# The first two products of a last second layer, taken as one two-level Strassen unit

## The chip, the cores and the metric

The kernel runs on one core of one Trainium2 chip. The metric is the device time of one execution in microseconds; the figure given for a kernel is the median of its runs. The profile times instructions on TensorE (PE, with PEld for its weight loads), VectorE (DVE), ScalarE (ACT), GpSimd (POOL) and on SyncE's queue (SP), which issues nearly all DMAs here.

## The reference

Eight batches of 576 tokens go through an efficient attention of eight heads; the result, as a 576 x 512 matrix x per batch, goes through a Fourier mixing block with a two-layer MLP:

```python
def _attn_ref(q, k, v):            # (8, 8, 576, 64) each
    q_s = softmax over the last axis;  k_s = softmax over the sequence axis
    kv = np.einsum('bhsd,bhse->bhde', k_s, v)
    return np.einsum('bhsd,bhde->bhse', q_s, kv)

def _moe_ref(x, w_ch1, w_ch2):     # x (8, 576, 512)
    mixed = np.real(fft(fft(x, axis=1), axis=2))
    u = x + mixed
    un = (u - mean(u)) / np.sqrt(var(u) + 1e-06)
    ch = np.maximum(un @ w_ch1, 0.0) @ w_ch2     # 512 -> 2048 -> 512
    return u + ch
```

All is fp32. This document is about the two matrix products of the MLP: the first layer (`un @ w_ch1`, then the ReLU) and the second layer (`@ w_ch2`).

## The kernel before

The 8 x 576 tokens are cut into nine groups of 512 rows. They are worked through in turn, and a group's place in the turn is called its order, 0 to 8 (B = 8). Each group has a first and then a second layer, and TensorE goes from one to the next without a break. This document needs **order 7** (`B - 1`) and **order 8** (`B`, the last).

**Strassen, one and two levels.** From order 1 on, each layer is done as the seven products of Strassen's scheme in Winograd's form instead of eight. A layer's left and right matrices are cut into 2 x 2 blocks; block sums ("sides") are made ahead, the seven products are numbered 1 to 7 and taken in the order `ORDER = (1, 6, 5, 7, 2, 4, 3)`, and their results are added up with running sums called s1, u2, u3. In the second layer products 1, 2 and 4 take raw blocks of the hidden layer and 7, 5, 6, 3 take sums of them; of the weights 1, 2 and 3 take raw blocks. Some products are cut once more in the same way, into seven sub-products; two products so treated together are a two-level *unit*.

- *First layer, order 7 and 8* (`wide_up`). Four *parts* j = 0..3, each for one pair of 128-row slices of the hidden layer in two halves. A part does products 1, 6, 7, 5 (`SHORT`) plainly, each as 8 matmuls of 128x256 in the records (line 1687). Products 2, 3 (and 4) are done for all parts at once as two-level units by `wide_unit`, seven sub-products of 8 matmul records of 128x128 each (line 1636). `WIDE` says which: `(2, 3)` in order 7, so there product 4 is done plainly in every part, and `(2, 3, 4)` in order 8. The TensorE order is part 0, the units, parts 1, 2, 3. A unit's results lie in the hidden layer's slots `WIDE_AT` until a part adds them (`more`, line 1698, on GpSimd). Then ReLU on ScalarE (line 1716), then the sides of the second layer (`side`, line 1701): slots 4, 2 on VectorE and 5, 6 on GpSimd, all four on VectorE for the last part.
- *Second layer, order 2 to 8* (`deep_down`). Order 7: product 1 plainly (`single`, line 1845: 32 matmul records of 128x256), then units (2, 4), (7, 6), (5, 3). Order 8: products 1 and 2 plainly, then units (7, 6), (5, 3), then product 4 plainly. A unit's sub-products (line 1875) are 16 matmul records of 128x128 for the two products together. VectorE makes a unit's sides (`a_step`, line 1821), adds up its results (`ends` and `plus`, line 1882), and adds results to x (`into`, line 1825; `add`, line 1856).

**PSUM.** Eight banks: one each named ba, bb, bc and one, and four that these layers do not use. Each of the first four has one buffer: a new group in a bank waits until what was in it has been read. The two-level units of the second layer put sub-products 1, 2 into ba, 6, 7, 4 into bb, 5, 3 into bc, so that a unit ends in bc and the next begins in ba.

**Weights.** They are streamed by SP through four slots of 1 MB, in the order of `self.plan`; `used(n)` frees a slot and issues the load of entry n + 4 (`load`, line 481). `w2d` in DRAM holds the ready sub-blocks of products 2 to 7, `w2s` the blocks for the plain form.

**Order of work.** Every step has a time written by hand, relative to its layer's begin (a part's or a unit's time is in nominal units, scaled by 0.87 for orders 1 to 8). All steps are sorted by it, and each engine does its own in that order; waits come from data dependencies alone. So an engine's queue is in strict order: an instruction that waits holds up all behind it on that engine. In order 8's first layer part 0 begins at 0, the units at 8, 15.2 and 22.4, parts 1 to 3 at 29.6, 37.6 and 45.6, the second layer at 53.6.

Of the kernel before, what the change touches and what calls it, by code (L numbers as in the profile page):

```python
# [141 lines left out]
class _Block:  # L142
    def __init__(self, ctx, tc, q, kT, v, w1, w2, ft, cd, out):
# [331 lines left out]
    def load(self, n):  # L475

        if n >= len(self.plan):
            return
        k = (n + 3) % 4
        w = self.big[:, k * NP * HD:(k + 1) * NP * HD]  # L480
        self.nc.sync.dma_start(w[:, :self.plan[n].shape[1]], self.plan[n])
        self.stream[n] = w.rearrange("p (a n) -> p a n", n=HD)
# [1132 lines left out]

    def wide_unit(self, g, m, e, *at_sums):
# [51 lines left out]
    def wide_up(self, order, g):  # L1668

        nc, V, G = self.nc, self.nc.vector, self.nc.gpsimd  # L1670
        base, wide = self.base[order], WIDE[order]
        products = [m for m in (*SHORT, 4) if m not in wide]
        size = 2 * len(products)

        def part(t, j, done):
# [3 lines left out]
            def product(m, i):  # L1679
                name = {1: "ba", 6: "bb", 7: "one", 5: "bc", 4: "one"}[m]  # L1680
                if i == 0 and m == 7:
                    box[name] = self.acc((P, D)).rearrange("p (j n) -> p j n", n=HD)
                elif i == 0 and m != 4:
                    box[name] = self.ps.tile([P, 2, HD], F32, tag=name, name=name)[:]
                w = self.stream[base + 2 * j + i]
                for k in range(2):
                    nc.tensor.matmul(box[name][:, i, :], lhsT=w[:, WA_AT[m], k * P:(k + 1) * P], rhs=self.unT[g][:, B_AT[m], k, :],  # L1687
                                     start=m != 4 and i == 0 and k == 0, stop=k == 1, skip_group_check=True)
# [8 lines left out]
            def more(to, of, m):  # L1697
                G.tensor_tensor(out=hp(to), in0=of(), in1=hp(WIDE_AT[m]), op=ALU.add)
# [7 lines left out]
            def late(m, i):  # L1706
                put(done[m] - t, more, i, own(i), m)
                put(done[m] - t + 1.6, relu, i)

            def sides(t, by_pool, last):  # L1710
                put(t, side, V, 4, 2, 3, ALU.add)
                put(t + 0.05, side, V, 2, 0, 2)
                put(by_pool, side, V if last else G, 5, 4, 0)
                put(by_pool + 0.1, side, V if last else G, 6, 1, 5)
# [4 lines left out]
            last, own_third = j == NP // 2 - 1, j == 0 and 4 in wide  # L1719
            for k, m in enumerate(products):  # L1720
# [4 lines left out]
            put(3.9, lambda: plus(temp("u2"), "bb", own(0) if j == 0 else got("s1")))  # L1725
            put(5.9, lambda: plus(hp(1) if own_third else temp("u3"), "one", got("u2")))
            put(7.9, lambda: plus(hp(3), "bc", own(1) if own_third else got("u3")))
            put(8.8, relu, 3)
            if j == 0:
                put(8.7, lambda: plus(hp(2), "bc", got("u2")))  # L1730
            else:
                put(4.7, lambda: more(WIDE_AT[3], got("u2"), 3))
                put(8.7, lambda: plus(hp(2), "bc", own(WIDE_AT[3])))
            if 4 not in wide:
                put(size - 0.1, lambda: plus(hp(1), "one", got("u2")))
                put(size + 0.7, relu, 1)
            if j == 0:
                put(1.9, lambda: nc.scalar.copy(hp(0), box["ba"]))
                for m, i in ((2, 0), (3, 2), (4, 1)):
                    if m in wide:  # L1740
                        late(m, i)
                t = max(done.values())
                sides(2.6, 3.4, False)
                return steps
            put(1.9, lambda: nc.scalar.copy(temp("s1"), box["ba"]))
            put(1.95, lambda: plus(hp(0), "ba", own(WIDE_AT[2])))
            put(2.8, relu, 0)
            if 4 in wide:
                put(6.7, lambda: more(1, got("u3"), 4))
                put(8.4 if last else size + 2.2, relu, 1)  # L1750
            put(9.5 if last and 4 in wide else size + 2.1 - 1.5 * last, relu, 2)
# [6 lines left out]
        t, units, done = size, [], {}  # L1758
        for k, m in enumerate(wide):
            e, times = (V, (-5.2, -5.1, -3.1, -3.0) if k else (-3.05, -3, -1.3, -1.2)) if order == B else (  # L1760
                G, [x - t + 0.1 * i for i, x in enumerate([10.1 if k else 0.5] * 4)])
            units += at(t, self.wide_unit(g, m, e, *times))
            t += UNIT
            done[m] = t + 0.5
        steps = part(0, 0, done) + units
        for j in range(1, NP // 2):
            steps += part(t, j, done)
            t += size
# [26 lines left out]
    def deep_down(self, g, order):  # L1795
# [4 lines left out]
        late, order = order == B - 2, (1, 2, *UNITS[1:], 4) if last else (1, *UNITS)  # L1800
# [3 lines left out]
        temps = {4: lambda i: un(i), 2: lambda i: un(3 + i), 7: self.gap, 6: dead(1), 5: (lambda i: un(i)) if last else dead(4), 3: (lambda i: un(3 + i)) if last else dead(2)}  # L1804
        result = {m: self.hblock(A_AT[m], 0, 0) for m in A_AT}
        tile = lambda m: result[m].rearrange("p (c e) n -> p c e n", c=2)
        box, steps, late_second = {}, [], not last and E is V
# [4 lines left out]
        def own(m):  # L1812
            def get(i):
                return temps[m](i - 4) if i > 3 else self.hblock(A_AT[m], i // 2, i % 2)
            return get

        def a_step(m, o):
# [3 lines left out]
            e.tensor_tensor(out=to(o), in0=to(x), in1=to(y), op=op)  # L1821
# [40 lines left out]
        place = {1: "ba", 2: "ba", 6: "bb", 7: "bb", 4: "bb", 5: "bc", 3: "bc"}  # L1862

        def product(unit, n, i):
            m = unit[i]
# [5 lines left out]
            if first:  # L1871
                bank(place[n])
            for f in range(4):
                r = q % 4 * 4 + f
                nc.tensor.matmul(box[place[n]][:, i, :], lhsT=own(m)(A_AT[n])[:, f, :],  # L1875
# [7 lines left out]

        def ends(unit, n):
            first, last = (A_AT[m] for m in unit)
            step = last - first
            out = lambda j: self.hpairs(j)[:, first:last + (1 if step > 0 else -1):step, 0:P]
            if n == 1:
                nc.scalar.copy(temp("s1"), box["ba"][:])
# [12 lines left out]
        after = {(2, 4): [(7, into, 1, 0, 4), (9, into, 0, 0, 2)],  # L1902
# [6 lines left out]
        for i, unit in enumerate(order):  # L1909
            if unit in A_AT:  # L1910
                w = base + (i if i < 2 else 2 + (len(DEEP) - skip) // 4)
# [15 lines left out]
            early = 6 if last and t < n + 8 else 0 if t == 8 else t - n + 2 if i == 2 else t - n + (0 if last else 3)  # L1927
            for k, o in enumerate((4, 5, 2, 6)):
                for j, m in enumerate(unit[::-1] if late_second and unit == (2, 4) else unit):
                    put(early + step * k + j * 1.1 + 0.3 + late * (i == 2), a_step, m, o)  # L1930
            for k, o in enumerate(ORDER):
                for j in range(2):
                    put(t + 2 * k + j, product, unit, o, j)
                put(t + 2 * k + 1.5, ends, unit, o)
            t += n
            for dt, *some in after[unit]:
                put(t + dt, *some)
        if last:
# [100 lines left out]
def kernel(ctx: ExitStack, tc: tile.TileContext, q, kT, v, w1, w2, ft,  # L2039
                                                           cd, out):  # L2040
    blk = _Block(ctx, tc, q, kT, v, w1, w2, ft, cd, out)

    ups = lambda order: len(WIDE[order]) * UNIT + 2 * (len(ORDER) - len(WIDE[order])) * (NP // 2) if order in WIDE else UP

    def timed(t, order, g):
# [5 lines left out]
        if order == B - 1:  # L2051
            steps += at(t, blk.wide_sums(3, blk.nc.gpsimd, 10.5, 10.6, 10.7, 10.8) + blk.wide_sums(4, blk.nc.gpsimd, 33, 34.6, 43, 44.6))
# [153 lines left out]
```

## Time and profile before

| | |
|---|---|
| median of 3 runs | 1004.52 us (1004.2 to 1005.18) |
| profiled execution, its own time | 1004.87 us |
| its span, first to last instruction | 1003.0 us |
| granted TensorE clock | 1.000 |
| busy: PE / PEld / DVE / ACT / POOL | 992.3 / 856.7 / 734.3 / 499.0 / 501.2 us |
| order 7, first and second layer | from 814 and from 862 us |
| order 8, first and second layer | from 907 and from 953 us |

Times in rows are microseconds from the span's start. In a timeline row stand the start, the length, the engine, the line, the operation, output and inputs by tile name, the shape and a count; in brackets the idle time before it and what ended it. Consecutive like instructions are merged into one row, so three of 0.6 us read as one row with x3. A matmul row's length holds the drain of its last matmul (0.16 us), so the next row starts before it ends.

### The profile page before, as it was taken

How to read it: one execution, taken by the hardware profiler on the slowest of the kernel's cores; microseconds unless marked ns; L12 is line 12 of the kernel's file. 1: busy time of each engine (PE TensorE's matmuls, PEld its weight loads, DVE VectorE, ACT ScalarE, POOL GpSimd, SP SyncE). 2: the span in 40 equal slices, each digit the busy share in tenths (PEclk: the TensorE clock that was granted, in tenths of full speed). 3: DMA queues.
4: the chain of work that ended last, by engine and by line, in shares of the span. 5: the costliest groups of instructions: out<-in, count | busy, mean ns of one | idle time of the engine just before them, and what ended most of it. 6: DMA issues, size and time to landing. Idle time of an engine off the chain costs nothing.

```text
span 1003.0 us, 20195 instructions
## 1 busy us (share of the span) xinstructions
PE 992.3 (99%) x7682; PEld 856.7 (85%) x7682; DVE 734.3 (73%) x1382; ACT 499.0 (50%) x1287; POOL 501.2 (50%) x492
## 2 busy tenths in 40 slices
PE   8999999999999999999999999999999999999998
PEld 7844464888888899889988998899888999999997
DVE  6898899666765887678756877688656956785673
ACT  5684643862468228842775167725782242252310
POOL 4363420357535637664655566665646396252510
PEclk9999999999999999999999999999999999999999
DMA  9986499687989666975778577947755964675473
GB/s 299 262 291 236 164 258 330 201 242 234 328 293 262 237 229 221 271 238 209 254 219 229 207 267 246 263 168 268 229 189 200 334 230 152 257 267 202 172 262 131
DMA packets 127256, 239.53 MB, mean 239 GB/s; under 512 B 24296, under 2 KB 92136, under 8 KB 116536
## 3 DMA queue, kind: packets, MB, share of 16 engines
q1 hardware_dynamic: 126792, 237.72, 72.5%
q8 instruction: 61, 1.00, 0.4%
q14 instruction: 35, 0.29, 0.1%
q10 hardware_dynamic: 288, 0.26, 0.1%
q0 software_dynamic: 80, 0.26, 0.1%
HBM read 203.08 MB, written 39.06 MB: 241 GB/s over the span
## 4 chain that ended last, share of the span: by engine, by line
PE 85%; DVE 8%; ACT 4%; issue 1%; DMA 1%; SPq 0%; POOL 0%; DVEq 0%; POOLq 0%
PE bb L1551 11%; PE bb L1875 10%; PE ba L1551 8%; PE bc L1551 7%; PE ba L1875 7%; PE bc L1875 7%; PE bb L1845 6%; PE bc L1484 2%; PE one L1687 2%; PE bb L1965 2%; PE two L845 2%; ACT qT L822 2%; PE two L1212 1%; PE two L1269 1%; PE one L760 1%; PE ba L1484 1%
## 5 line engine op out<-in xcount | busy, mean ns | idle before, releaser
L1551 PE MATMUL bb<-unT,big 128*128 128x256 f32 x576 | 137.8, 381 | 0.0
L1551 PEld LDWEIGHTS bb<-unT,big 128*128 128x128 f32 x576 | 108.4, 190 | 15.5 <-DVE u L1519 0.5
L822 ACT ACTIVATE qT<-q 32x128 f32<-32x128 f32 x384 | 117.9, 307 | 5.9 <-DVE q L812 0.8
L1875 PE MATMUL bb<-big 128*128 128x128 f32 x848 | 103.8, 276 | 0.2
L1875 PEld LDWEIGHTS bb<-big 128*128 128x128 f32 x848 | 98.9, 192 | 1.0 <-DVE u L1882 1.0
L1551 PE MATMUL ba<-unT,big 128*128 128x256 f32 x384 | 93.7, 383 | 0.0
L1551 PE MATMUL bc<-unT,big 128*128 128x256 f32 x384 | 91.2, 380 | 0.1
L1825 POOL TENSOR_TENSOR x<-x,big 128x512 f32<-128x512 f32 x45 | 60.7, 1363 | 46.0 <-DVE big L1882 19.7
L1563 ACT ACTIVATE big<-big 128x512 f32<-128x512 f32 x72 | 44.7, 629 | 77.9 <-DVE big L1562 71.3
L1551 PEld LDWEIGHTS bc<-unT,big 128*128 128x128 f32 x384 | 72.5, 190 | 10.4 <-DVE big L1562 0.5
L1519 DVE TENSOR_TENSOR u<-bb,s 128x512 f32<-128x512 f32 x50 | 34.2, 684 | 64.4 <-PE bb L1551 45.9
L1551 PEld LDWEIGHTS ba<-unT,big 128*128 128x128 f32 x384 | 71.3, 190 | 10.6 <-issue 0.5
L1821 DVE TENSOR_TENSOR big<-big 128x512 f32<-128x512 f32 x98 | 79.7, 840 | 0.0
L1875 PE MATMUL ba<-big 128*128 128x128 f32 x640 | 79.0, 276 | 0.0
L1875 PEld LDWEIGHTS ba<-big 128*128 128x128 f32 x640 | 75.0, 192 | 0.8
L809 POOL TENSOR_TENSOR q<-q,qm 128x512 f32<-128x512 f32 x24 | 25.8, 1074 | 89.1 <-DVE qm L804 55.4
L1395 POOL COPY unT<-unT 32x256 f32<-32x256 f32 x98 | 44.1, 450 | 48.1 <-DVE unT L1387 43.8
L1395 ACT COPY unT<-unT 32x256 f32<-32x256 f32 x126 | 50.7, 402 | 31.5 <-DVE unT L1387 29.7
L410 POOL TENSOR_TENSOR big<-big 128x512 f32<-128x512 f32 x24 | 30.5, 1270 | 67.2 <-ACT big L1563 67.2
L1845 PE MATMUL bb<-big 128*128 128x256 f32 x256 | 58.3, 379 | 0.0
L1845 PEld LDWEIGHTS bb<-big 128*128 128x128 f32 x256 | 48.0, 190 | 6.1
L1875 PE MATMUL bc<-big 128*128 128x128 f32 x416 | 50.7, 275 | 0.0
(410 smaller groups left out, 2211.6 us busy)
## 6 DMA issues: line engine op xcount, KB each, us to landing
big<-w2d SPq DMA_DIRECT2D x67, 1024.0 KB
big<-w1s SPq DMA_DIRECT2D x64, 896.0 KB
big<-w2s SPq DMA_DIRECT2D x16, 1024.0 KB
big<-in_w_dram SPq DMA_DIRECT2D x21, 512.0 KB
w2d<-big SPq DMA_DIRECT2D x42, 256.0 KB
kb<-in_kT_dram SPq DMA_DIRECT2D x28, 320.0 KB
q<-in_q_dram SPq DMA_DIRECT2D x28, 256.0 KB
vt<-in_v_dram SPq DMA_DIRECT2D x84, 80.0 KB
```

The costliest lines, as they stand in the source:

```text
L410: e1.tensor_tensor(out=to(4), in0=at(2), in1=at(3), op=ALU.add)
L809: G.tensor_tensor(out=heads(), in0=heads(), in1=m[:].unsqueeze(2).to_broadcast([P, H, DH]), op=ALU.add)
L822: nc.scalar.activation(to[t, i * Q:i * Q + Q], one, ACT.Exp)
L1395: copy(to, of)
L1484: nc.tensor.matmul(po[:], lhsT=h[:, f, i * P:(i + 1) * P], rhs=self.w2sb[:, f, :], start=(f == 0), stop=(f == NF - 1))
L1519: plus = lambda t: V.tensor_tensor(out=temp(t), in0=box["bb"][:], in1=box["s1"][:], op=ALU.add)
L1551: nc.tensor.matmul(bank()[:, i, :], lhsT=w[:, WA_AT[m], k * P:(k + 1) * P], rhs=self.unT[g][:, B_AT[m], k, :], start=first and i == 0 and ...
L1563: (0.8, lambda: nc.scalar.activation(hp(i), hp(i), ACT.Relu))]
L1821: e.tensor_tensor(out=to(o), in0=to(x), in1=to(y), op=op)
L1825: E.tensor_tensor(out=x, in0=x, in1=tile(m), op=ALU.add)
L1845: nc.tensor.matmul(box[name][:, i, :], lhsT=h[p][:, A_AT[m], i * P:(i + 1) * P], rhs=self.stream[n][:, p, :], start=p == 0 and (m != 1 or ...
L1875: nc.tensor.matmul(box[place[n]][:, i, :], lhsT=own(m)(A_AT[n])[:, f, :], rhs=w[:, r // 2, r % 2 * P:r % 2 * P + P], start=first and f == ...
```

## The change

1. **Order 7, first layer.** `WIDE` becomes a list in which parts and units are mixed: `(0, 0), 2, 3, (0, 1), 4, (0, 2), (0, 3)`. Product 4 is a two-level unit there too, between parts 1 and 2. Its weight sides (`wide_sums(4)`, GpSimd) come some 17 nominal units sooner; its activation sides are made by VectorE. Order 8's list is as it was.
2. **First layers of both orders.** `WIDE_AT` puts the units' results in other slots; the times of `sides` are changed, partly by the table `SIDES`; in the last part the addition of product 4 (`more`) moves from GpSimd to VectorE, and its ReLU comes 0.8 sooner. In order 8 the last part's sides come 1.9 later.
3. **Order 8, second layer.** Products 1 and 2 become a two-level unit (1, 2). Its sub-products come in the order `RAW_FIRST = (1, 4, 2, 6, 5, 7, 3)`: 1, 4, 2 take raw blocks of the hidden layer. Sub-product 4 gets bank one and 3 gets bank ba. The unit's eight side steps are on VectorE at 1.55 to 1.7 and 7.6 to 9.7; those of unit (7, 6) begin at 8.3.
4. **Weights for it.** Product 2's come as two stream entries from `w2d`, taken at every other sub-block (2 KB pieces). Product 1's raw block is loaded into `kb` at 16.2 of order 8, and VectorE makes its four sums at 23.2, 25.9, 32.4 and 36.35 (`last_first`).
5. Unit (2, 4) of order 7 makes its sides in the order 2, 4 instead of 4, 2 (`late_second` is gone).

```diff
+RAW_FIRST = (1, 4, 2, 6, 5, 7, 3)
-UNIT, WIDE_AT = 7.2, {2: 5, 3: 6, 4: 4}
-WIDE = {B - 1: (2, 3), B: (2, 3, 4)}
+UNIT, WIDE_AT = 7.2, {2: 4, 3: 5, 4: 6}
+WIDE = {B - 1: ((0, 0), 2, 3, (0, 1), 4, (0, 2), (0, 3)), B: ((0, 0), 2, 3, 4, (0, 1), (0, 2), (0, 3))}
+SIDES = {(B - 1, 0): (25.2, 32, 31, 41), (B - 1, 1): (33.2, 35.2, 34.2, 45.9), (B, 0): (25.1, 28.05, 26.5, 31.7)}
...
-            self.plan += [one(m) for m in (ORDER if at == 1 else (1, 2) if at == B else (1,))]
+            if at == B:
+                self.plan += [self.w2d[:, i:j:2, :] for i, j in ((0, 8), (8, 2 * len(ORDER)))]
+            else:
+                self.plan += [one(m) for m in (ORDER if at == 1 else (1,))]
...
+    def last_first(self, *times):
...
+        def load():
+            raw = kb[:, 0:4 * GT]
+            self.nc.sync.dma_start(raw, self.w2s[WB_AT[1]].rearrange("p a n -> p (a n)"))
...
+        def make(o, x, y):
+            V.tensor_tensor(out=w[o], in0=w[x], in1=w[y], op=ALU.subtract)
+        some = (4, 1, 0), (1, 3, 1), (5, 3, 4), (6, 2, 5)
+        return [(times[0], load)] + [(t, lambda a=a: make(*a)) for t, a in zip(times[1:], some)]
...
-            def more(to, of, m):
-                G.tensor_tensor(out=hp(to), in0=of(), in1=hp(WIDE_AT[m]), op=ALU.add)
+            def more(to, of, m, e=G):
+                e.tensor_tensor(out=hp(to), in0=of(), in1=hp(WIDE_AT[m]), op=ALU.add)
...
-                put(4.7, lambda: more(WIDE_AT[3], got("u2"), 3))
+                put(5.2, lambda: more(WIDE_AT[3], got("u2"), 3))
...
+                put(6.7, lambda: more(1, got("u3"), 4, V if last else G))
+                put(7.6 if last else size + 2.2, relu, 1)
             if last:
-                sides(size + 2.6, size + 3.4, True)
+                late = 1.9 * (order == B)
+                sides(*(size + late + dt for dt in (2.6, 2.65, 3.4, 3.5)), True)
+            elif (order, j) in SIDES:
+                sides(*(x - t for x in SIDES[order, j]))
             else:
-                sides(size + (3.95 if 4 in wide else 2.3), size + (8.3 if 4 in wide else 3), False)
+                sides(size + 2.8, size + 4.75, size + 3.7, size + (6.7 if j == NP // 2 - 2 else 8.2))
...
+        if order == B:
+            steps += self.last_first(16.2, 23.2, 25.9, 32.4, 36.35)
...
-        late, order = order == B - 2, (1, 2, *UNITS[1:], 4) if last else (1, *UNITS)
+        late, order = order == B - 2, ((1, 2), *UNITS[1:], 4) if last else (1, *UNITS)
...
+        def place(unit, n):
+            return {4: "one", 3: "ba"}.get(n, "bb" if n in (6, 7) else "bc" if n == 5 else "ba") if unit == (1, 2) else {1: "ba", 2: "ba", 6: "bb", 7: "bb", 4: "bb", 5: "bc", 3: "bc"}[n]
+        def raw_first(unit, n, i):
...
+        def ends_raw(n, out):
+            if n == 1:
+                nc.scalar.copy(temp("s1"), box["ba"][:])
+            if n == 6:
+                plus(temp("u2"), "bb", "s1")
+            if n == 7:
+                plus(temp("u3"), "bb", "s1")
+                plus(out(3), "bc", "u3")
+                plus(out(2), "one", "u3")
+            if n == 2:
+                nc.scalar.copy(out(0), box["ba"][:])
+            if n == 5:
+                plus(box["u2"][:], "bc", "u2")
+            if n == 3:
+                plus(out(1), "ba", "u2")
...
-            early = 6 if last and t < n + 8 else 0 if t == 8 else t - n + 2 if i == 2 else t - n + (0 if last else 3)
-            for k, o in enumerate((4, 5, 2, 6)):
-                for j, m in enumerate(unit[::-1] if late_second and unit == (2, 4) else unit):
+            early = 8 if last and t < n + 8 else 0 if t == 8 else t - n + 2 if i == 2 else t - n + (0 if last else 3)
+            if unit == (1, 2):
+                for m, at_steps in ((1, (1.55, 1.65, 7.6, 9.6)), (2, (1.6, 1.7, 7.7, 9.7))):
+                    for o, dt in zip((4, 5, 2, 6), at_steps):
+                        put(dt, a_step, m, o, V)
+            for k, o in enumerate((4, 5, 2, 6) if unit != (1, 2) else ()):
+                for j, m in enumerate(unit):
                     put(early + step * k + j * 1.1 + 0.3 + late * (i == 2), a_step, m, o)
-            for k, o in enumerate(ORDER):
+            for k, o in enumerate(RAW_FIRST if unit == (1, 2) else ORDER):
                 for j in range(2):
                     put(t + 2 * k + j, product, unit, o, j)
-                put(t + 2 * k + 1.5, ends, unit, o)
+                put(t + 2 * k + 1.5 + 3 * (unit == (1, 2) and o == 2), ends, unit, o)
...
-            steps += at(t, blk.wide_sums(3, blk.nc.gpsimd, 10.5, 10.6, 10.7, 10.8) + blk.wide_sums(4, blk.nc.gpsimd, 33, 34.6, 43, 44.6))
+            steps += at(t, blk.wide_sums(3, blk.nc.gpsimd, 10.5, 10.6, 10.7, 10.8) + blk.wide_sums(4, blk.nc.gpsimd, 15.8, 23, 23.1, 27.2))
```

More of the change, by code (lines that the diff above doesn't have):

```diff
@@ L1670, in wide_up, with part @@
         nc, V, G = self.nc, self.nc.vector, self.nc.gpsimd
[L1671 to L1675, printed above, removed]
+        base, size = self.base[order], 2 * len(SHORT)
+        def part(t, j):
+            pending = {m for m in done if done[m] > t + UNIT}
             hp = lambda i, h=self.hpairs(j, 2): h[:, :, i, :]
@@ L1718, in part @@
             own = lambda i: lambda: hp(i)
-            last, own_third = j == NP // 2 - 1, j == 0 and 4 in wide
-            for k, m in enumerate(products):
+            last, third = j == NP // 2 - 1, own(1) if 4 in pending else got("u3")
+            for k, m in enumerate(SHORT):
                 for i in range(2):
@@ L1745, in part @@
[L1745 to L1751, printed above, removed]
+                put(9.5 if last or 4 in pending else size + 2.1, relu, 2)
+            if 4 in pending:
+                late(4, 1)
+            else:
+                put(6.7, lambda: more(1, got("u3"), 4, V if last else G))
+                put(7.6 if last else size + 2.2, relu, 1)
@@ L1756, in part @@
             return steps
[L1758 to L1762, printed above, removed]
-            t += UNIT
[L1764 to L1768, printed above, removed]
+        done, t, steps = {}, 0, []
```

121 lines of the change are left out of this document (87 added, 34 removed).

## The prediction, made before the changed kernel was run

> **What bounds the kernel now.** I read the page first: the shares of busy time, then the chain that ended last.
>
> ```profile
> PE 992.3 (99%) x7682; PEld 856.7 (85%) x7682; DVE 734.3 (73%) x1382; ACT 499.0 (50%) x1287; POOL 501.2 (50%) x492
> PE 85%; DVE 8%; ACT 4%; issue 1%; DMA 1%; SPq 0%; POOL 0%; DVEq 0%; POOLq 0%
> ```
>
> TensorE is the bound, and an average of 99% says that time is won only by giving it less to do, and lost wherever it has to wait. So I read TensorE's timeline from 813 us on (orders 7 and 8) for starts that come later than the row before allows.
>
> ```profile
> 813.96 1.89 PE L1687 MATMUL ba<-unT,big 128*128 128x256 f32 x8
> ...
> 819.14 1.89 PE L1687 MATMUL bc<-unT,big 128*128 128x256 f32 x8
> 821.56 1.99 PE L1687 MATMUL one<-unT,big 128*128 128x256 f32 x8 [0.52 <-DVE unT L1410]
> ...
> 861.84 7.07 PE L1845 MATMUL bb<-big 128*128 128x256 f32 x32
> ...
> 906.67 1.89 PE L1687 MATMUL ba<-unT,big 128*128 128x256 f32 x8
> 908.40 1.89 PE L1687 MATMUL bb<-unT,big 128*128 128x256 f32 x8
> ...
> 930.55 1.06 PE L1636 MATMUL bb<-big,qT 128*128 128x128 f32 x8
> 931.44 1.06 PE L1636 MATMUL bc<-unT,T 128*128 128x128 f32 x8
> ...
> 946.15 1.89 PE L1687 MATMUL ba<-unT,big 128*128 128x256 f32 x8
> ...
> 953.06 7.07 PE L1845 MATMUL bb<-big 128*128 128x256 f32 x32
> 959.97 3.62 PE L1845 MATMUL bc<-big 128*128 128x256 f32 x16
> ...
> 966.87 1.95 PE L1875 MATMUL ba<-big 128*128 128x128 f32 x16
> 968.66 1.95 PE L1875 MATMUL bb<-big 128*128 128x128 f32 x16
> ...
> 977.59 1.95 PE L1875 MATMUL bc<-big 128*128 128x128 f32 x16
> 979.38 1.95 PE L1875 MATMUL ba<-big 128*128 128x128 f32 x16
> ```
>
> Starts give the prices. A plain product of a second layer takes 959.97 - 953.06 = 6.91 us; a group of a part 908.40 - 906.67 = 1.73; a unit's sub-product 931.44 - 930.55 = 0.89 in the first layer and 968.66 - 966.87 = 1.79 for two products in the second; a unit of two products 979.38 - 966.87 = 12.51, which is 6.25 for one. **A product made two-level saves 0.65 us.** The change does it three times: 1.96 us, just 0.2% of the run. 0.2% (2.0 us) is also about what a measurement of this kernel can tell from no change. So the question is how many waits the change removes or makes.
>
> **Order 7's first layer.** It takes 861.84 - 813.96 = 47.88. Changed, it has the instructions of order 8's, which runs without a wait in 953.06 - 906.67 = 46.39. That is 1.49 less: product 4, and the wait at 821.56 (0.69 after 819.14 + 1.73). Product 4 needed the last activation block, and this is now read only after part 1. What is late next is that all behind comes 2.5 us sooner:
>
> ```profile
> 821.43 1.27 DVE L1691 TENSOR_TENSOR big<-bc,u 128x512 f32<-128x512 f32 x2
> ...
> 825.73 1.26 POOL L1611 TENSOR_TENSOR F<-ft 128x512 f32<-128x512 f32 x1
> 827.07 1.27 POOL L1611 TENSOR_TENSOR cd<-F 128x512 f32<-128x512 f32 x1
> ```
>
> Unit 2 would start at 819.14 + 1.73 = 820.87 and want bank bc two sub-products later, at 822.65; its readers end at 821.43 + 1.27 = 822.70: 0.1. Unit 3 would start at 820.87 + 6.25 + 0.1 = 827.2 and want its second weight sum (cd) one sub-product later, at 828.1; GpSimd has it at 828.34 and has no gap ahead: 0.3. Part 1 then ends at 840.7 and unit 4 wants bc 1.79 later. GpSimd must by then have done the ReLU input of slot 2, three weight sums and part 1's `more`, five jobs of 1.27 from 834.8 (unit 3's end at 833.8, its last result, the hand-over): 841.2, with VectorE's second read of bc behind it. With some mutual slowing (next part) that costs 0 to 0.5; I take 0.2. Before unit 4's last sub-product reuses bc (5.36 in), VectorE's queue holds seven jobs: the two reads of bc, side, u2, side, u3, and the read that frees bc. At 0.61 each with the last one 0.72 behind u3 that is 4.4 us, with both sides slowed by GpSimd 5.5: 0 to 0.6, I take 0.35. In all 0.95 of new waits, 0.4 to 1.6: **-0.54, from -1.1 to +0.1**.
>
> **Order 8's first layer: VectorE in unit 4.** TensorE's list is the old one, but two VectorE jobs, part 0's slot 4 side (25.1) and the second sum of `last_first` (25.9), now stand ahead of u3 (26.36). The side waits for part 0's ReLU of slot 2, and that for GpSimd.
>
> ```profile
> 927.12 1.27 POOL L1698 TENSOR_TENSOR big<-big 128x512 f32<-128x512 f32 x1 [4.98 <-DVE big L1645]
> 928.43 0.63 ACT L1716 ACTIVATE big<-big 128x512 f32<-128x512 f32 x1 [0.66 <-POOL big L1698]
> 929.86 0.69 DVE L1645 TENSOR_TENSOR u<-one,u 128x512 f32<-128x512 f32 x1 [1.04 <-PE one L1636]
> 930.58 0.69 DVE L1645 TENSOR_TENSOR big<-bc,u 128x512 f32<-128x512 f32 x1
> 839.10 1.41 DVE L1701 TENSOR_TENSOR big<-big 128x512 f32<-128x512 f32 x2
> 840.42 0.68 DVE L1691 TENSOR_TENSOR u<-bb,s 128x512 f32<-128x512 f32 x1
> ```
>
> Now bc is read until 931.27 and its last sub-product starts at 931.44: 0.17 us of slack. Changed, the side cannot start before 928.43 + 0.63 = 929.06. Two such jobs hold VectorE for 840.42 - 839.10 = 1.32, so u3 starts at 930.4, bc's reader 0.72 later and ends at 931.8: a wait of 0.4. The first sum of `last_first` (23.2) runs beside the GpSimd row and may delay it by some 0.3, so I take **+0.65**, with 0 (the sum finds a gap) and 1.2 as ends.
>
> **Order 8's second layer, its begin.** Before: 966.87 - 953.06 = 13.81 for products 1 and 2; as a unit 12.51, a gain of 1.30. Product 2's slot was wanted 6.9 us into the layer; now the second half of the first sub-product wants it at 953.06 + 0.89 = 953.95. Ahead of its ReLU (0.63) stands the addition that VectorE now does, two SBUF inputs, while GpSimd works off part 3's `more` and a side:
>
> ```profile
> 950.41 2.36 DVE L1701 TENSOR_TENSOR big<-big 128x512 f32<-128x512 f32 x2
> 952.69 0.68 DVE L1691 TENSOR_TENSOR u<-one,u 128x512 f32<-128x512 f32 x1
> 950.58 1.65 POOL L1698 TENSOR_TENSOR big<-u,big 128x512 f32<-128x512 f32 x1 [0.17 <-DVE u L1691]
> 819.95 1.55 DVE L1410 TENSOR_TENSOR unT<-unT 128x512 f32<-128x512 f32 x1
> ```
>
> Two sides that take 1.32 elsewhere took 2.36 beside GpSimd, and a single job 1.55. u3 starts between 951.5 (its group's end, 946.15 + 3 x 1.73 + 0.16) and 952.7 (as now). The addition follows 0.72 later and takes 0.68 to 1.55, then the ReLU: 953.6 to 955.6, a wait of 0 to 1.7. I take u3 at 951.8 (one side is now done sooner) and an addition of 1.3 in part beside GpSimd: 954.5, **+0.55**. The Trainium skill (SBUF — State Buffer, "Who interferes with whom") speaks against moving this addition: VectorE with two SBUF inputs contends with a GpSimd instruction that reads SBUF, and the loser blocks for the whole instruction. The 1.55 us row agrees with contention, though not with a full block of 1.27 + 0.68; by the rule this wait would be some 0.6 more.
>
> **The same unit, its end.** Sub-product 3 is put into bank ba, and so is the first of unit (7, 6). TensorE must wait until VectorE has read it. At the old border (977.59 bc, 979.38 ba) the banks differ and there is no gap. The Trainium skill (Perfetto Trace Analysis, "Optimizing Tensor Performance") asks for just that: independent groups should rotate through banks, so that reading one overlaps the next; by it this border costs at least one read.
>
> What the wait costs is VectorE's queue, which is strict. Behind sub-product 6's end stand, by their times: u2 (7.5), two sides (7.6, 7.7), two of unit (7, 6) (8.3, 9.4), u2 again (9.5), two sides (9.6, 9.7), one of (7, 6) (11.3), u3 and two results (11.5), one of (7, 6) (12.4), and then the read of ba (13.5).
>
> ```profile
> 963.96 1.89 DVE L1821 TENSOR_TENSOR big<-big 128x512 f32<-128x512 f32 x3
> 970.71 0.42 DVE L1882 TENSOR_TENSOR u<-bb,s 128x256 f32<-128x256 f32 x1 [0.21 <-PE bb L1875]
> 986.72 0.42 DVE L1882 TENSOR_TENSOR u<-bb,s 128x256 f32<-128x256 f32 x1 [1.75 <-PE bb L1875]
> 987.18 0.42 DVE L1882 TENSOR_TENSOR big<-bc,u 128x256 f32<-128x256 f32 x1
> 987.52 0.68 DVE L1825 TENSOR_TENSOR x<-x,big 128x512 f32<-128x512 f32 x1
> ```
>
> A side is (1.89 - 0.68) / 2 = 0.605 in a run; a result 0.34 before an independent job, 0.46 before one that needs it, 0.42 at the end. Eight sides 4.84, four results at 0.34 and u3 at 0.46 1.82, the last 0.42: 7.08. The queue starts 0.10 after sub-product 6 ends (968.66 + 1.95 to 970.71), which is 4 x 1.79 + 0.16 = 7.31 into the unit (its own sides are no limit: the addition's end at 953.9, two results at 0.61 and four sides at 0.605 give 957.5, and it is wanted at 958.4). With 0.05 for the hand-over, unit (7, 6) starts 7.31 + 0.10 + 7.08 + 0.05 = 14.54 after the layer's begin, plus the 0.55 above. Against 13.81: **+0.73**. If the queue were empty it would be 12.51 + 0.16 + 0.10 + 0.42 + 0.05 = 13.24, that is -0.57. Behind it VectorE has the 12.5 us of unit (7, 6) for some 8 us of work and catches up; units (7, 6), (5, 3), product 4 and the last stores follow as before.
>
> **At nothing.** `last_first`'s other sums lie in part 1, where no bank is short; ScalarE is idle for most of it. On SP the new 1 MB load waits for unit 2, done at 920 by then, and `kb` is read 6 us later (0.87 x 23.2 after 906.67); the stream entries for the unit are issued as before (below), 7 us ahead of the layer. If one landed late TensorE would wait by as much.
>
> ```profile
> 945.48 1.21 SPq L481 DMA_DIRECT2D big<-w2s x2
> ```
>
> **Sum.** -0.54 + 0.65 + 0.55 + 0.73 = +1.39. The profiled execution (1004.87, a span of 1003.0 and 1.9 around it) would be 1006.3; it stood 0.35 above the median, so I say 1004.5 + 1.4 = 1005.9.
>
> **Rivals.** They are weighed with VectorE's load at this place:
>
> ```profile
> 953.20:967.00 13.80, 13.80 (x67) 12.15 (x66) 10.02 (x16) 2.25 (x4) 3.87 (x4) 1.00 0.64 240
> ```
>
> *The saving comes through*: VectorE runs ahead in all these places, GpSimd is in time but for cd, only ba's reader counts: -1.49 + 0.4, 0, and -0.57: -1.7, 1002.8; with the cd wait gone too, just over -2.0. For it: VectorE (10.02 us busy, the third engine of the row) is idle for 3.8 of the 13.8 us now. Against: the rows above, by queue order. Chance 0.25. *GpSimd and VectorE hold each other up throughout*: the waits at their upper ends, +0.1, +1.2, +1.0 and 0.73: +3.0, 1007.5. It decides from the point where part 3's addition on VectorE ends after 954.3. For it: the 2.36 row is in just this place. Chance 0.2. *A weight load is late*: pieces of 2 KB, or the `kb` load among the output stores; a wait of about 2 us on top of the forecast, 1007.9. The same queue has fed plain products in time so far. Chance 0.05. My forecast (+0.4 to +2.2): 0.5.
>
> **The numbers.** Faster by over 0.2% (under 1002.5) is only the edge of the first rival: 0.06. Slower by over 0.2% (over 1006.5) is the second and third and a little of the forecast's edge: 0.29. Within: 0.65. The range 1003.0 to 1007.5 leaves out the first rival's far edge and the third.
>
> **What would show it.** In the changed profile: a row for unit (7, 6)'s first ba group 14.5 to 15.5 after the layer's begin, with a wait for VectorE's read of ba (the sum `ends_raw` for 3); a short wait half-way in the layer's first group, for ScalarE; a wait of 0.4 to 0.9 before order 8's last unit-4 group; order 7's first layer at 47.3. I am wrong if unit (7, 6) starts under 13.3 in, or if order 7's first layer takes 46.5.

## The result, and the profile after

The changed kernel is slower: 1007.28 us (1006.03 to 1009.37, 15 runs) against 1004.72 for the kernel before in the same runs; the ratio is 1.0026, 95% interval 1.0020 to 1.0033. That is +2.6 us, where +1.4 was forecast and 1003.0 to 1007.5 was the range.

The begin of order 7 lies between 813.1 and 816.5 us in the eleven profiles of the changed kernel and of the experiments, though the stages ahead of it are not changed. So the stages are compared by their lengths, from the start of their first TensorE group to the start of the next stage's:

| stage | before | after | difference | forecast |
|---|---|---|---|---|
| order 7, first layer | 47.88 | 48.89 | +1.01 | -0.54 |
| order 7, second layer | 44.83 | 44.86 | +0.03 | 0 |
| order 8, first layer | 46.39 | 47.13 | +0.74 | +0.65 |
| order 8, products 1 and 2 | 13.81 | 14.49 | +0.68 | +1.28 |
| order 8, units (7, 6), (5, 3) | 25.01 | 25.12 | +0.11 | 0 |
| sum | 177.92 | 180.49 | +2.57 | +1.39 |

The lengths add up to the measured difference. TensorE's timeline of the changed kernel shows where they grow; here L1716 is a part's product, L1666 a sub-product in the first layer, L1889 a plain product, L1921 a sub-product of unit (1, 2) for one of the two products, L1939 one of the other units.

```profile
813.43 1.89 PE L1716 MATMUL ba<-unT,big 128*128 128x256 f32 x8
...
840.28 1.06 PE L1666 MATMUL ba<-unT,vt 128*128 128x128 f32 x8
841.17 1.06 PE L1666 MATMUL bb<-big,qT 128*128 128x128 f32 x8
843.91 1.13 PE L1666 MATMUL bc<-big,qT 128*128 128x128 f32 x8 [1.69 <-DVE big L1720]
...
862.32 7.07 PE L1889 MATMUL bb<-big 128*128 128x256 f32 x32
...
907.18 1.89 PE L1716 MATMUL ba<-unT,big 128*128 128x256 f32 x8
...
932.59 1.16 PE L1666 MATMUL bc<-unT,T 128*128 128x128 f32 x8 [0.47 <-DVE big L1675]
...
954.31 1.05 PE L1921 MATMUL ba<-kb,big 128*128 128x128 f32 x8
955.20 1.06 PE L1921 MATMUL ba<-big 128*128 128x128 f32 x8
...
964.13 1.06 PE L1921 MATMUL bb<-big,qT 128*128 128x128 f32 x8
965.63 1.13 PE L1921 MATMUL ba<-kb,unT 128*128 128x128 f32 x8 [0.44 <-DVE unT L1865]
966.60 1.06 PE L1921 MATMUL ba<-big,unT 128*128 128x128 f32 x8
968.80 2.05 PE L1939 MATMUL ba<-big 128*128 128x128 f32 x16 [1.15 <-DVE big L1946]
```

Four new waits of 0.4 us or more, all for VectorE: 1.69 before unit 4 of order 7 reuses bank bc, 0.47 at the end of unit 4 of order 8, 0.44 and 1.15 at the end of unit (1, 2). The wait for the last activation block (821.56 before) is gone; unit (7, 6) starts 14.49 us into the layer, the forecast's 14.54 without its extra wait.

The largest is in the place where 0.2 was forecast. VectorE's and then GpSimd's timelines there (L1657 rows are the four activation sums of unit 4, L1720 the reads of part 1's banks, L1730 a side, L1620 a weight sum, L1727 an addition of a unit's result):

```profile
837.98 0.76 DVE L1657 TENSOR_TENSOR big<-unT 128x128 f32<-128x128 f32 x1
838.78 1.24 DVE L1657 TENSOR_TENSOR big<-unT,big 128x128 f32<-128x128 f32 x1
839.94 0.68 DVE L1720 TENSOR_TENSOR big<-one,u 128x512 f32<-128x512 f32 x1
840.54 0.75 DVE L1657 TENSOR_TENSOR big<-unT 128x128 f32<-128x128 f32 x1
841.22 1.35 DVE L1657 TENSOR_TENSOR big<-unT,big 128x128 f32<-128x128 f32 x1
842.49 1.27 DVE L1720 TENSOR_TENSOR big<-bc,big 128x512 f32<-128x512 f32 x2
...
836.87 1.73 POOL L1620 TENSOR_TENSOR q<-vt,q 128x512 f32<-128x512 f32 x1
838.55 1.32 POOL L1620 TENSOR_TENSOR T<-vt,qT 128x512 f32<-128x512 f32 x1
839.83 1.31 POOL L1727 TENSOR_TENSOR big<-u,big 128x512 f32<-128x512 f32 x1
841.11 1.32 POOL L1730 TENSOR_TENSOR big<-big 128x512 f32<-128x512 f32 x1
```

GpSimd's addition is done at 841.14. Counted from the layer's begin that is 27.71, 0.47 later than forecast (841.2 - 813.96 = 27.24), but still 0.9 before TensorE wants bc (841.17 + 0.89 = 842.06). The reads of bc end at 842.49 + 1.27 = 843.76 all the same. The four 128x128 sums, which take 0.28 to 0.29 us each with GpSimd idle (first experiment), took 0.76, 1.24, 0.75 and 1.35 beside it, and all stand ahead of these reads in VectorE's queue.

### The profile page after: what moved, and what is told of

The parts are those of the page before. It is cut to its first block, busy times and chain, and to the rows that moved or that the text cites. A ratio compares the mean times of both kernels' runs of the same rounds, so it can differ in the third digit from the quotient of the medians.

```text
span 1005.1 us, 20377 instructions
## 1 busy us (share of the span) xinstructions
PE 990.7 (99%) x7754; PEld 857.9 (85%) x7754; DVE 751.0 (75%) x1406; ACT 499.5 (50%) x1290; POOL 503.3 (50%) x494
## 4 chain that ended last, share of the span: by engine, by line
PE 86%; DVE 9%; DMA 2%; issue 1%; ACT 1%; POOL 0%; SPq 0%; DVEq 0%; POOLq 0%
PE bb L1560 12%; PE bb L1939 10%; PE ba L1560 8%; PE bc L1560 8%; PE ba L1939 7%; PE bc L1939 7%; PE bb L1889 4%; PE bc L1493 2%; PE bb L2054 2%; PE two L854 2%; PE one L769 2%; PE two L1221 1%; PE two L1278 1%; PE ba L1493 1%; PE ba L1716 1%; PE bc L2054 1%
## 5 line engine op out<-in xcount | busy, mean ns | idle before, releaser
L1939 PE MATMUL bb<-big 128*128 128x128 f32 x840 | 102.9, 276 | 0.3 <-DVE u L1946 0.2
L1939 PEld LDWEIGHTS bb<-big 128*128 128x128 f32 x840 | 98.0, 192 | 1.0 <-DVE u L1946 1.0
L1939 PE MATMUL ba<-big 128*128 128x128 f32 x640 | 79.1, 276 | 1.1 <-DVE big L1946 1.1
L1939 PEld LDWEIGHTS ba<-big 128*128 128x128 f32 x640 | 75.0, 192 | 2.1 <-DVE big L1946 1.3
L1404 POOL COPY unT<-unT 32x256 f32<-32x256 f32 x98 | 43.4, 443 | 46.6 <-DVE unT L1396 42.3
L1939 PE MATMUL bc<-big 128*128 128x128 f32 x400 | 48.9, 275 | 0.0
L1889 PE MATMUL bb<-big 128*128 128x256 f32 x208 | 47.7, 379 | 0.0
L1939 PEld LDWEIGHTS bc<-big 128*128 128x128 f32 x400 | 46.8, 192 | 0.0
```

The lines of the kernel that those rows point to most:

```text
L1404: copy(to, of)
L1889: nc.tensor.matmul(box[name][:, i, :], lhsT=h[p][:, A_AT[m], i * P:(i + 1) * P], rhs=self.stream[n][:, p, :], start=p == 0 and (m != 1 or ...
L1939: nc.tensor.matmul(box[place(unit, n)][:, i, :], lhsT=own(m)(A_AT[n])[:, f, :], rhs=w[:, r // 2, r % 2 * P:r % 2 * P + P], start=first and ...
```

## The experiments

Each run is an edit of the changed kernel: the move of a job, a bank or a few jobs, or several of these together. Each ratio is to runs of the kernel before that were taken beside it, so compare ratios, not medians. Waits and lengths are from the profiles. In the diffs, `...` stands for code left out.

**Unit 4's activation sums of order 7, sooner.**

```diff
-... 4: (-5.2, -5.1, -3.1, -3.0) if order == B else (-3.2, -3.1, -1.2, -1.1)}[some]
+... 4: (-5.2, -5.1, -3.1, -3.0) if order == B else (-8.9, -8.8, -7.9, -7.8)}[some]
```

> The changed kernel, but the four activation sums of order 7's unit 4 (VectorE, 128x128) are made some five nominal units sooner, beside the end of unit 3, where GpSimd has a gap. Theory A (these sums, slowed by GpSimd from 0.29 to 0.75-1.35 us each, stand ahead of the reads of bank bc in VectorE's queue): TensorE's 1.69 us wait at the third sub-product of unit 4 goes, at most 0.3 is left, order 7's first layer takes 47.0 to 47.4 us instead of 48.89, and the whole is 1.5 to 1.9 us faster than the changed kernel. Rival B (the read of bc waits for GpSimd's own addition, which comes late because of its three weight sums): the wait stays at 1.3 us or more and the first layer above 48.4.

Measured: 1005.92 us, ratio to the kernel before 1.0011 (1.0002 to 1.0020). Order 7's first layer took 861.38 - 814.20 = 47.18, and the wait is gone but for 0.16 (842.98 - 841.93 = 1.05, where 0.89 is free of waits). Theory A, not B:

```profile
833.99 0.28 DVE L1657 TENSOR_TENSOR big<-unT 128x128 f32<-128x128 f32 x1
834.31 0.29 DVE L1657 TENSOR_TENSOR big<-unT,big 128x128 f32<-128x128 f32 x1
...
842.14 0.69 DVE L1720 TENSOR_TENSOR big<-bc,big 128x512 f32<-128x512 f32 x1 [0.21 <-POOL big L1727]
...
842.98 1.13 PE L1666 MATMUL bc<-big,qT 128*128 128x128 f32 x8
```

Now the read does wait for GpSimd's addition, but 0.21 us: rival B's wait is real, and it was the small one.

**A side on GpSimd later, VectorE's queue untouched.**

```diff
-SIDES = {(B - 1, 0): (25.2, 32, 31, 41), ...
+SIDES = {(B - 1, 0): (25.2, 32, 35, 41), ...
```

> The changed kernel, but GpSimd makes part 0's slot 5 side of order 7 behind part 1's, so that it does not run beside VectorE's fourth activation sum; VectorE's queue is as it was. Theory A with contention as the price: the fourth sum takes 0.3 to 0.5 us instead of 1.35, the wait at unit 4 falls from 1.69 to 0.6-0.8 and order 7's first layer to 47.8-48.1 us. Rival C (the number of jobs in VectorE's queue costs the time, not their slowing): the wait stays within 0.2 of 1.69. Rival B: the wait stays too, as GpSimd's addition is not moved.

Measured: 1006.90 us, ratio 1.0021 (1.0012 to 1.0030); order 7's first layer 862.22 - 814.42 = 47.80, the wait 0.61. With the same jobs in the same order, only the fourth sum is faster:

```profile
839.74 1.24 DVE L1657 TENSOR_TENSOR big<-unT,big 128x128 f32<-128x128 f32 x1
...
842.19 0.28 DVE L1657 TENSOR_TENSOR big<-unT,big 128x128 f32<-128x128 f32 x1
```

So contention is the price (rival C falls): taking one of the two longest sums out of GpSimd's way shortens it by 1.07 and gives back 1.08 of the 1.69 us.

**A bank of its own for sub-product 3 of unit (1, 2).**

```diff
+            ... {4: "one", 3: "three"}.get(n, ...
...
+            elif first and n == 3:
+                box["three"] = self.two()[:, 0, 0:HD].rearrange("p (a n) -> p a n", n=P)
...
-                plus(out(1), "ba", "u2")
+                plus(out(1), "three", "u2")
```

> The changed kernel, but sub-product 3 of unit (1, 2) is put into a PSUM bank that nothing else uses in this stage, so that unit (7, 6) need not wait for the read of ba. Theory A (bank ba is what TensorE waits for): unit (7, 6) starts 13.0 to 13.3 us after the layer's begin instead of 14.49 (0.44 of wait for the sides of sub-product 3 stays), and no later group waits by more than 0.2; 1.1 to 1.3 us faster than the changed kernel. Rival D (VectorE's load in this stage is the bound, whatever the bank): the wait turns up again within unit (7, 6), at its second or third group, and the start of unit (5, 3) is earlier by less than 0.5.

Measured: 1007.49 us, ratio 1.0024 (1.0015 to 1.0034). Unit (7, 6) starts 969.15 - 956.03 = 13.12 in, as theory A says, but then waits, and unit (5, 3) starts 26.49 in instead of 27.10. That is 0.61 sooner, half of what A expected and more than the 0.5 that D allowed. A later group waits 0.59, as D said and A did not, though at the unit's fourth group:

```profile
969.15 1.95 PE L1941 MATMUL ba<-big 128*128 128x128 f32 x16
...
973.62 1.06 PE L1941 MATMUL bc<-big,F 128*128 128x128 f32 x8
975.27 2.05 PE L1941 MATMUL bb<-big 128*128 128x128 f32 x16 [0.59 <-DVE u L1948]
```

VectorE's u2 of unit (7, 6), for which it waits, starts 974.80 - 956.03 = 18.77 in; in the changed kernel it was 973.07 - 954.31 = 18.76. The bank did nothing to VectorE's queue, which has no gap from sub-product 6 of unit (1, 2) to behind this u2.

**Two sides of unit (7, 6) behind the read of ba.**

```diff
+                    put({(5, 0): 13.6, (5, 1): 13.7}.get((o, j), dt) if last and unit == (7, 6) else dt, a_step, m, o)
```

> The changed kernel with bank ba kept, but two of unit (7, 6)'s side steps (the second of each product) stand behind the read of ba in VectorE's queue instead of ahead of it. Theory A (the strict queue ahead of the read sets the wait): the read of ba ends about 0.5 us after sub-product 3's end, unit (7, 6) starts 13.5 to 13.8 us into the layer instead of 14.49, and its second group does not wait; 0.7 to 1.0 us faster. Rival D (VectorE's load is the bound): the wait moves on to unit (7, 6)'s second group, which needs these sides, and the start of unit (5, 3) is earlier by less than 0.3.

Measured: 1007.58 us, ratio 1.0029 (1.0018 to 1.0041). Unit (7, 6) starts 13.86 in, near A's range, but unit (5, 3) 982.61 - 955.75 = 26.86: 0.24 sooner, rival D's number. What was won comes back, not at D's second group but at the fourth, for the same u2 (975.36 - 974.18 = 1.18, where 0.89 is free of waits). Theory A explains where the wait stands, not how much is lost. That led to theory E: the queue runs without a gap, and a wait goes only when jobs that are not yet due stand behind those that are.

**VectorE's queue in the order of what is due, bank ba kept; then with the bank.** Unit (7, 6)'s sides go behind the results of unit (1, 2); two additions to x and two sides of unit (5, 3) go behind u2 of unit (7, 6). No job is removed. With the bank of its own, unit (7, 6)'s four times are 9.75, 9.8, 11.3 and 11.4, the rest is the same.

```diff
-        after = {(1, 2): [(0.3, into, 0, 0, 1), (0.9, into, 0, 0, 2)], ...
+        after = {(1, 2): [(4.6, into, 0, 0, 1), (4.7, into, 0, 0, 2)], ...
...
+                    moved_to = {(7, 6): {(4, 0): 12.4, (4, 1): 13.55, (5, 0): 13.6, (5, 1): 13.65}, (5, 3): {(4, 0): 18.5, (4, 1): 18.55}} if last else {}
...
-                half(t + 1.6, 0, 0, 0)
-                half(t + 2.4, 1, 0, 0)
+                half(t + 5.6, 0, 0, 0)
+                half(t + 6.4, 1, 0, 0)
```

> The changed kernel with bank ba kept, but VectorE's queue in order 8's second layer is put in the order in which results are due: unit (7, 6)'s sides stand behind the results of unit (1, 2) where they can, and two additions to x and two sides of unit (5, 3) stand behind unit (7, 6)'s u2. No job is taken away. Theory E (VectorE's queue runs without a gap, so a wait that is removed in one place comes back at the next result that is due, until jobs that are not yet due are moved behind): unit (7, 6) starts 13.2 to 13.5 us into the layer instead of 14.49, no later group waits, and unit (5, 3) starts 25.7 to 26.0 in instead of 27.10. Rival D (VectorE's load, whatever the order): unit (5, 3) starts 26.6 or later.

> As the kernel with the queue in due order, but sub-product 3 also has a PSUM bank of its own. Theory E: with the order right the bank now pays in full: unit (7, 6) starts 12.5 to 12.7 us into the layer and unit (5, 3) 25.0 to 25.3, which is the whole 1.3 us that the two-level unit saves in TensorE time against the kernel before (13.81 and 26.32). Rival D: unit (5, 3) starts 26.2 or later, as with the bank alone.

Measured, bank kept: 1006.69 us, ratio 1.0016 (1.0007 to 1.0025); unit (7, 6) starts 967.20 - 954.02 = 13.18 in, unit (5, 3) 25.95. With the bank: 1006.46, ratio 1.0013 (1.0004 to 1.0022); 967.86 - 955.35 = 12.51 and 25.16. Both as theory E says, within 0.02 us. The bank alone gave 0.61 us at the start of unit (5, 3), the order alone 1.15, both 1.94. TensorE's rows of the first of the two show the one wait that is left, which is for the read of ba:

```profile
965.63 1.06 PE L1921 MATMUL ba<-big,unT 128*128 128x128 f32 x8
967.20 2.05 PE L1939 MATMUL ba<-big 128*128 128x128 f32 x16 [0.52 <-DVE big L1946]
```

**Order 8's unit 4: two VectorE jobs behind the read of bc.**

```diff
-SIDES = {... (B, 0): (25.1, 28.05, 26.5, 31.7)}
+SIDES = {... (B, 0): (26.5, 28.05, 26.7, 31.7)}
...
-            steps += self.last_first(16.2, 23.2, 25.9, 32.4, 36.35)
+            steps += self.last_first(16.2, 23.2, 26.6, 32.4, 36.35)
```

> The changed kernel, but in order 8's unit 4 VectorE's slot 4 side of part 0 and the second sum for unit (1, 2) stand behind u3 and the read of bank bc instead of ahead of them. Theory A (these two jobs, of which the first waits for ScalarE, delay the read of bc): the 0.47 us wait and the gap around it at the last sub-product of unit 4 go, and order 8's first layer takes 46.4 to 46.6 us instead of 47.13; nothing else moves. Rival D (VectorE has too much to do there): the wait turns up again at part 1's second or fourth group and the layer stays above 46.9.

Measured: 1007.92 us, ratio 1.0028 (1.0016 to 1.0040). The layer took 954.90 - 907.67 = 47.23: no gain. The wait moved on to part 1's second group, as rival D said; VectorE's rows tell why:

```profile
932.79 0.68 DVE L1641 TENSOR_TENSOR kb<-kb 128x512 f32<-128x512 f32 x1
933.39 1.75 DVE L1730 TENSOR_TENSOR big<-big 128x512 f32<-128x512 f32 x1
935.07 0.68 DVE L1675 TENSOR_TENSOR big<-bb,u 128x512 f32<-128x512 f32 x1
...
935.80 1.99 PE L1716 MATMUL bb<-unT,big 128*128 128x256 f32 x8 [0.57 <-DVE big L1675]
```

The read that frees bb (935.07) now stands behind the two jobs and a third, a side that takes 1.75 us beside GpSimd where 0.68 is usual.

**All moves together; then with unit 4's three jobs each behind what it would delay.**

```diff
+SIDES = {... (B, 0): (28.45, 29.5, 29.6, 31.7)}             # the second of the two
...
+            steps += self.last_first(16.2, 23.2, 29.45, 32.4, 36.35)
```

> All moves together: order 7's activation sums sooner, order 8's two VectorE jobs behind u3, unit (1, 2) with a bank of its own and the queue in due order. If the waits are independent of each other: order 7's first layer 47.0 to 47.4 us (before the change 47.88), order 8's first 46.4 to 46.6 (46.39), unit (5, 3) 25.0 to 25.3 into the second layer (26.32); in all 1.6 to 2.2 us less than the kernel before the change, 1002.4 to 1003.0 where that takes 1004.6. If one wait's removal feeds another, the sum is short by 0.5 us or more.

> All moves, but in order 8's unit 4 the side of slot 4, the second sum for unit (1, 2) and the side of slot 2 each stand behind the last read of a bank that they would delay (slot 4's side behind the read of bb, the other two behind the read of bc). Theory E (a wait goes only when every job not yet due stands behind what is due): the 0.57 us wait at part 1's second group goes, order 8's first layer takes 46.4 to 46.6 us instead of 47.23, order 7's first layer and the second layer stay at 47.2 and 25.2, and the whole is 1.8 to 2.3 us below the kernel before (ratio 0.9977 to 0.9982). Rival D (VectorE has too much to do there in any order): the layer stays above 46.9, with the wait at part 1's later groups.

Measured, first: 1004.03 us, ratio 0.9988 (0.9979 to 0.9997); order 7's first layer 47.19, order 8's first 47.23 (the wait of the experiment above, where 46.4 to 46.6 was expected), unit (5, 3) 25.16 in. Second: 1003.80 us where the kernel before took 1004.67, ratio 0.9987 (0.9978 to 0.9996), short of the expected ratio; order 7's first layer 47.16, order 8's first 952.63 - 906.24 = 46.39, so rival D falls there, unit (5, 3) 977.96 - 952.63 = 25.33. In these stages it is 1.71 us under the kernel before; of that the medians show 0.9, and the interval holds both. The profiled spans (1001.9 and 1003.0) differ by 1.1: in this execution order 7 began 0.26 later, and from unit (5, 3)'s start to the end, the last stores included, it took 23.94 instead of 23.62. Whether that part belongs to the kernel or to the execution stays open. Here a wait at the unit's begin turned up, 0.17 us:

```profile
952.63 1.05 PE L1923 MATMUL ba<-kb,big 128*128 128x128 f32 x8
953.52 1.24 PE L1923 MATMUL ba<-big 128*128 128x128 f32 x8
954.59 1.06 PE L1923 MATMUL one<-q,big 128*128 128x128 f32 x8
```

**GpSimd's sums for unit 3 ahead of its additions to x** (in order 7, added to the second kernel above):

```diff
-... enumerate([0.5 if some == 2 else 10.1] * 4)]
+... enumerate([0.5 if some == 2 or order == B else 3.4] * 4)]
...
-... blk.wide_sums(3, blk.nc.gpsimd, 10.5, 10.6, 10.7, 10.8) ...
+... blk.wide_sums(3, blk.nc.gpsimd, 3.81, 3.82, 3.83, 3.84) ...
```

> As the kernel with everything in due order, and in order 7 GpSimd makes the activation and weight sums of unit 3 ahead of its five additions to x instead of behind them. If unit 3's short wait for its second weight sum is GpSimd's queue order, it goes (0.13 us) and order 7's first layer takes 46.9 to 47.1 us instead of 47.2; if the additions to x, now later, hold up something else, the layer takes 47.3 or more.

Measured: 1010.64 us, ratio 1.0059 (1.0045 to 1.0073); a miss, and a dear one: the first layer took 867.91 - 813.86 = 54.05.

```profile
826.64 0.69 DVE L1720 TENSOR_TENSOR big<-bc,u 128x512 f32<-128x512 f32 x1 [4.99 <-POOL x L1869]
...
827.48 2.05 PE L1666 MATMUL bc<-big,kb 128*128 128x128 f32 x8 [4.77 <-DVE big L1720]
829.32 1.91 PE L1666 MATMUL one<-big,kb 128*128 128x128 f32 x8
831.03 1.71 PE L1666 MATMUL ba<-unT,kb 128*128 128x128 f32 x8
```

The additions to x read the last group's results out of the hidden layer's slots, and the read of bc writes part 0's result into such a slot. Not only data but room is due on time. The wait is not the whole price: the three sub-products behind it took 1.84, 1.71 and 1.54 us from start to start instead of 0.89, 2.4 us more, in a stretch (827.48 to 832.57) in which the granted clock was 0.52; from 832.57 on it was 1.00 again.

## Why the prediction was right, point by point

**The bound and the prices held.** TensorE's saving in unit (1, 2) is what was worked out: with the waits taken away, it takes 12.51 us. The change turns slower by waits for VectorE, as forecast. That the total lies in the range, 0.2 us under its upper end, is partly luck: order 7's first layer lost 1.55 us more than forecast, outside the range given for it, and order 8's unit (1, 2) 0.60 less.

**Order 7's first layer: right mechanism, wrong size.** The step that failed is the wait for bc in unit 4, "five jobs of 1.27" on GpSimd and "With some mutual slowing (next part) that costs 0 to 0.5; I take 0.2". GpSimd was in time. The forecast priced the read of bc by GpSimd alone and left the four activation sums of unit 4 out of VectorE's queue ahead of it. Slowed by GpSimd, they cost 1.7 us, which the first two experiments gave back wholly and in part. The waits for bc in unit 2 and for cd in unit 3 were there, at 0.17 and 0.14 where 0.1 and 0.3 were forecast: unit 2's third group starts 822.29 - 821.23 = 1.06 after the second where 0.89 is free of waits, and unit 3's second 827.86 - 826.83 = 1.03. The wait of 0.35 at unit 4's end shrank to nothing, as TensorE was already late.

**Order 8's unit 4: right.** +0.74 for +0.65, with the chain as told:

```profile
929.25 0.63 ACT L1745 ACTIVATE big<-big 128x512 f32<-128x512 f32 x1 [0.98 <-POOL big L1727]
...
929.92 0.69 DVE L1730 TENSOR_TENSOR big<-big 128x512 f32<-128x512 f32 x1 [0.58 <-ACT big L1745]
930.52 0.68 DVE L1641 TENSOR_TENSOR kb<-kb 128x512 f32<-128x512 f32 x1
931.13 0.69 DVE L1675 TENSOR_TENSOR u<-one,u 128x512 f32<-128x512 f32 x1
931.85 0.69 DVE L1675 TENSOR_TENSOR big<-bc,u 128x512 f32<-128x512 f32 x1
```

ReLU, side, sum, u3, read of bc, one behind the other, and the group at 932.59 after it.

**Unit (1, 2)'s begin: the 0.55 us did not come.** Counted from the layer's begin, VectorE's addition ended at 0.62 (954.93 - 954.31), near the forecast's 0.76 (951.8 + 0.72 + 1.3 - 953.06). By the forecast's rule a wait of 0.40 was still due (955.60 - 955.20, below), and there was none:

```profile
953.88 1.05 DVE L1727 TENSOR_TENSOR big<-u,big 128x512 f32<-128x512 f32 x1
...
954.97 1.83 ACT L1745 ACTIVATE big<-big 128x512 f32<-128x512 f32 x3 [3.43 <-DVE big L1727]
```

The first ReLU ends at about 955.6, and the forecast had the group wanting it at its start, 955.20. But by the kernel each of its four pairs of matmuls reads one part's rows, and only the last pair reads part 3's: an estimate of 955.20 + 6 x 0.112 = 955.87. In the second kernel with all moves the first ReLU ended 1.59 into the layer instead of 1.29, about when the last pair wanted it (1.56), and the group took 0.17 longer (the row of 1.24 above). The step that failed is "the second half of the first sub-product wants it at 953.06 + 0.89 = 953.95".

**Unit (1, 2)'s end: right in size, half right in cause.** 14.49 for 14.54, and the read of ba is what TensorE waits for; the queue ahead of it, counted job by job, gave the number to 0.05 us. The 0.44 us that sub-product 3 waits for its own sides was not forecast ("its own sides are no limit"); it adds nothing here, as the read of ba comes later still (968.33, sub-product 3 ends at 967.66), but it is there in the run with the bank alone, as 0.35. But "VectorE ... catches up" was too easy: it catches up only after u2 of unit (7, 6), so that neither the bank nor two moved sides alone bring back the 1.2 us. The bank's rule in the Trainium skill (Perfetto Trace Analysis, "Optimizing Tensor Performance") holds: the wait for the read of ba is there with the bank kept and gone with a bank of its own. The traces put its share, once the queue is in order, at 13.18 - 12.51 = 0.67 us; the two runs also differ in where unit (7, 6)'s sides stand, so this is not the bank's share alone.

**The first rival, "the saving comes through", failed by the order of jobs, not by their number.** VectorE does the same work in the two kernels with all moves together, and the two-level unit then takes 12.50 and 12.68 us, near the 12.51 that the rows promised.

**The other rivals.** The second, GpSimd and VectorE hold each other up throughout, has the total nearest to the measured one (+3.0 for +2.6), but not its stages. It put +0.1 on order 7's first layer and +1.7 on unit (1, 2), where +1.01 and +0.68 were measured, and its sign, an addition that ends 1.24 into the layer or later (954.3 - 953.06), did not come: 0.62. What it names is real, but in one place, unit 4 of order 7. The third, a late weight load, did not show: from order 7 on, all waits of TensorE that the profile names are for VectorE.

## What to carry to other kernels

Where one engine's queue is in strict order and without gaps, removing the wait that the trace names moves it to the next result that is due: sort that queue by what the bound engine needs next, and only then spend a bank or a buffer. When a step is brought forward, price every instruction of each queue between the old and the new place, small ones too, and price those that start beside a GpSimd instruction by what may be left of it. A job that looks as if it could wait may be what frees the room for another.

## What was not expected of the hardware

In these rows a VectorE instruction with two inputs in SBUF that starts while GpSimd runs one of its own does not run slowly throughout: its end follows GpSimd's end by a fixed time, as if it stood until then. From the changed kernel, VectorE's and GpSimd's timelines:

```profile
951.81 1.44 DVE L1730 TENSOR_TENSOR big<-big 128x512 f32<-128x512 f32 x1
...
951.43 1.27 POOL L1730 TENSOR_TENSOR big<-big 128x512 f32<-128x512 f32 x1 [1.50 <-DVE big L1730]
952.66 1.72 POOL L1727 TENSOR_TENSOR big<-u,big 128x512 f32<-128x512 f32 x1
```

The side ends at 953.25, 0.55 after GpSimd's 952.70; the addition at 953.88 ends at 954.93, 0.55 after 954.38; the four 128x128 sums end 0.14, 0.15, 0.15 and 0.14 after the GpSimd instructions in which they start (838.60, 839.87, 841.14 and 842.43). The read of bank one at 839.94, with one input in SBUF, took its usual 0.68 while GpSimd ran. The forecast had read 1.55 us as a partial slowing; these rows make the price what is left of GpSimd's instruction when VectorE's starts, less about 0.15, whatever the size of VectorE's own: 1.06 us for the sum at 841.22 (1.35 - 0.29), 0.37 for the addition at 953.88 (1.05 - 0.68). So "some 0.6 more" at unit (1, 2)'s begin, worked out from a whole GpSimd instruction, was too much.

The Trainium skill (SBUF — State Buffer, "Who interferes with whom") calls the port pair that the two engines share an exclusive lock, and says of VectorE's two-port modes that whoever issues first has it for the whole instruction and the other fully blocks. By the same section `tensor_tensor` has no such mode but contends when both its inputs are in SBUF. The rows above, all `tensor_tensor`, agree with a full block.
